# Routing attention and a MetaFormer MLP on one core: every softmax sum joined to one half before its matmul, tiny weights told by a minimum, and rows of x of two sequences made inside the MLP

## The chip, the cores and the metric

The program runs on one core of a Trainium2 chip. The metric is device time in microseconds, from the first instruction of the program to its end; the lower it is, the better. The core has TensorE (PE in the profile; PEld is its weight loads), VectorE (DVE), ScalarE (ACT), GpSimd (POOL) and SyncE (SP). SP computes nothing here: it issues most of the DMA transfers, one after the other in its program order.

## The reference

```
q, k, v: (4, 8, 768, 64) float32      centroids: (8, 16, 64)
q_assign, k_assign = argmax over 16 centroids of the normalized rows
mask   = q_assign[:, :, :, None] == k_assign[:, :, None, :]
scores = where(mask, q @ k^T / 8, -1e9);  attn = exp(scores - max) / (sum + 1e-9)
x      = (attn @ v) with the 8 heads side by side: (4, 768, 512)
xn     = (x - mean) / sqrt(var + 1e-6) * g_ln
out    = x + relu(xn @ w_ch1) @ w_ch2     w_ch1: 512x2048, w_ch2: 2048x512, both float64
```

## The kernel before

**Attention.** The 4 sequences by 8 heads make 16 pairs of heads, numbered n = 0 to 15 (four pairs to a sequence b). A pair is worked in two units, one for each half of the queries (`slot` 0 and 1). In a unit PE makes six score tiles of 128 keys by 2x384 queries in PSUM, ACT takes their exponential into a tile `e` in SBUF, and PE multiplies `e` by v (L398). VectorE adds the six tiles of a unit up: `add_up` adds three `e` tiles of two steps each (L433, L436), which leaves two halves of 128x768, `two[:, 0]` and `two[:, 1]`. `finish(n, 0)` multiplies the sums by a matrix of ones on PE (`den_ps`, L452), four matmuls with 32 columns of weights for each half, so that the denominators of a pair come out in one PSUM bank. For the pairs in `NARROW` = (7, 8, 9, 10, 14) VectorE joins the two halves first (L438), and PE has four such matmuls instead of eight; pair 15 has its own path and four. The order of PE, DVE, ACT and POOL is written out by hand here (`manual_schedule`); SP's is left to the scheduler.

`finish(n, 1)` takes the reciprocal of the denominators through DRAM; `finish(n, 2)` multiplies and stores x by columns (`xT_d`); `finish(n, 3)` transposes it on DVE (L498) and stores rows (`x_d`) with four DMAs of 128-byte pieces.

**The weights** are float64 in DRAM. They come as 32 chunks m of 128x512 (16 of w1, then 16 of w2). For each, SP loads the raw words (L242, two buffers, so that the load of chunk m+2 follows the last reading of chunk m), DVE splits off the high words and joins the low ones, and POOL adds the low part onto the weight with an accumulating DMA (L274). In `split_weight` DVE makes `ta` (L251, L254) and the masked exponent `tb` (L257); in `join_weight` it multiplies `ta` by (exponent >= SMALLEST), so that tiny weights become 0 (L266), and scales the low words (L270, L271). Chunks 0 to 21 are converted within the attention: two in each of the pairs 0 to 6 (`TWICE`) and one in each of the pairs 7 to 14. The other ten are converted within the first layer of the MLP for sequence 0, at the places that `within` gives.

**The MLP** treats w1 and w2 as 2x2 blocks and makes seven products where eight would be needed (Strassen's scheme in Winograd's form), with sums on DVE. `first_layer(b, j, part)` makes one of the seven products of hidden chunk pair j = 0 to 7; a run of seven such products is called unit j here. `product` (L803) writes PSUM banks `x_ps`, `y_ps`, `z_ps`; ACT copies x out (L829) and DVE adds y or z to the copy (`add_relu`, L834). `w1_sums` (L627) makes the block sums of w1 for the unit that follows. The last three of unit 7 stand thus:

```
        if tt == 0:
            first_layer(0, NFH - 1, 4)
            first_layer(0, NFH - 1, 3)
```

that is, behind the first 16 matmuls of the second layer (`second_layer`, L910; seven products, each over three row tiles tt). Part 3 adds onto the `z_ps` bank that DVE has to have read for part 7 before. Sequences 1 to 3 then have a first layer like that of sequence 0 and a second layer in a deeper scheme (`deep_layer`, L1093). `w2_whole(False)` stores w2 to DRAM in 16 pieces (L1001, `w_all<-w`), each as soon as the four chunks that it holds have been accumulated; those stores and the raw loads are on the same SP queue, in an order that the scheduler makes. During the second layer of sequence 0 only PE's order is written by hand; the scheduler orders DVE. There DVE makes sums of hidden tiles (`hidden_sums`), sums of w2 (`w2_sum`), adds x to the results (`add_rows`, with a load `xb` of rows of x) and normalizes sequence 1 (`norm_rows`, `norm_apply`, `x_sum`).

At the end a flag (`all_in_range`) chooses whether a slow general path, after the end of the measured work, has to redo everything. With this data it doesn't.

Of the kernel before, what the change touches and what calls it, by code (L numbers as in the profile page):

```python
# [15 lines left out]
PSUM = bass.MemoryType.PSUM  # L16


@with_exitstack
def kernel(  # L20
# [20 lines left out]
    Q = 32  # L41
# [35 lines left out]
    TWICE = 7  # L77

    NARROW = (7, 8, 9, 10, 14)
# [143 lines left out]
    halves = {}  # L223
# [20 lines left out]

    def split_weight(m):
        words = raws[m].bitcast(U32).rearrange("p (n w) -> p n w", w=2)
        hi = words[:, :, 1]
        ta = pools["conv"].tile([P, WC], U32, tag="ta", name="ta")
        tb = pools["conv"].tile([P, WC], U32, tag="tb", name="tb", bufs=2)

        nc.vector.tensor_scalar(  # L251
            ta, hi, 0x07FFFFFF, 3, op0=ALU.bitwise_and, op1=ALU.logical_shift_left
        )
        nc.vector.scalar_tensor_tensor(  # L254
            out=ta, in0=hi, scalar=0xC0000000, in1=ta, op0=ALU.bitwise_and, op1=ALU.bitwise_or
        )
        nc.vector.tensor_single_scalar(tb, hi, 0x7FF00000, op=ALU.bitwise_and)  # L257
        halves[m] = (ta, tb)

    def join_weight(m):  # L260
        lo = raws.pop(m).bitcast(U32).rearrange("p (n w) -> p n w", w=2)[:, :, 0]
        ta, tb = halves.pop(m)
        fa, fb = ta.bitcast(F32), tb.bitcast(F32)
        w = weight_chunk(m)[1]

        nc.vector.scalar_tensor_tensor(  # L266
            out=w, in0=tb, scalar=float(0x38100000), in1=fa, op0=ALU.is_ge, op1=ALU.mult
        )

        nc.vector.tensor_single_scalar(tb, w.bitcast(U32), 0xFF800000, op=ALU.bitwise_and)  # L270
        nc.vector.scalar_tensor_tensor(  # L271
            out=fb, in0=lo, scalar=2.0 ** -52, in1=fb, op0=ALU.mult, op1=ALU.mult
        )
        nc.gpsimd.dma_start(out=w, in_=fb, accum_op=ALU.add)  # L274
# [141 lines left out]
    def add_up(n, g, parts=range(2)):  # L416
# [17 lines left out]
        if 1 in parts:  # L434
            two = sums[n, g]
            nc.vector.tensor_tensor(two, two, soft.pop(u + 2), ALU.add)  # L436
            if n in NARROW:
                nc.vector.tensor_tensor(two[:, 0], two[:, 0], two[:, 1], ALU.add)  # L438
            sums[n, g] = [two[:, h] for h in range(1 if n in NARROW else 2)]
# [3 lines left out]
    def finish(n, part):  # L443
# [39 lines left out]
        elif part == 2:  # L483
            a, x = xs.pop(n), late[n]
            if b:
                nc.vector.tensor_tensor(x, a, x, ALU.mult)
                nc.sync.dma_start(out=xT_d[b][pr], in_=x)
            else:
                late[n] = norm_tiles(b)[0][:, pr, :]
                nc.vector.tensor_tensor(late[n], a, x, ALU.mult)  # L490
        else:
            x = late.pop(n)

            if n + 1 < len(pairs):
                y = last.tile([P, S], F32, tag="y", name="y")
            else:
                y = late["all"][:, 0]
            nc.vector.transpose(y, x)  # L498
            for i in range(P // Q):
                m = pr * P + i * Q  # L500
                nc.sync.dma_start(
                    out=x_d[b].rearrange("t (a r) m -> r (t a) m", r=Q)[:, :, m : m + Q],
                    in_=y[i * Q : (i + 1) * Q].rearrange("r (g f) -> r g f", f=Q),
                )
# [153 lines left out]
    for n in range(len(pairs) - 1):  # L658
        for slot in (0, 1) if n < TWICE else (0,):
            convert[n, slot] = len(convert)  # L660
# [98 lines left out]
    def all_in_range():  # L759
# [8 lines left out]
        for op, op1 in ((ALU.max, ALU.is_le), (ALU.min, ALU.is_ge)):  # L768
            nc.vector.tensor_reduce(ends[:, 1:2], hits, AX.X, op)
            nc.vector.tensor_single_scalar(ends[:, 1:2], ends[:, 1:2], float(NG), op=op1)  # L770
            nc.vector.tensor_tensor(ends[:, 0:1], ends[:, 0:1], ends[:, 1:2], ALU.min)
# [24 lines left out]
    for m in range(len(convert), NWC):  # L796
        within.setdefault((1, 2, 2, 3, 4, 4, 5, 6, 6, 7)[m - len(convert)], []).append(m)
# [98 lines left out]
    def hidden_sums(c, late):  # L896

        a11, a12, a21, a22 = [hidden[r, l, c] for r in range(2) for l in range(2)]
        if late:
            nc.vector.tensor_tensor(a12, a12, a11, ALU.subtract)  # L900
            return
        s3 = place("e")[:, c]
        hidden["s3", c] = s3
        nc.vector.tensor_tensor(s3, a11, a21, ALU.subtract)
        nc.vector.tensor_tensor(a21, a21, a22, ALU.add)
        nc.vector.tensor_tensor(a11, a21, a11, ALU.subtract)
# [10 lines left out]
    def add_rows(b, r, tt, j, bank):  # L917
# [3 lines left out]
        o = early.tile([P, MH], F32, tag="o", name="o_sb", bufs=12)  # L921
# [70 lines left out]
    def w2_whole(back):  # L992

        for r in range(2):
            for k in range(2):
                for l in range(2):
                    for h in range(2):
# [3 lines left out]
                        nc.sync.dma_start(out=w if back else d, in_=d if back else w)  # L1001
# [318 lines left out]
    with tc.manual_schedule(engines={mybir.EngineType.PE}):  # L1320
# [5 lines left out]
        relu(len(summed))  # L1326
        w2_sum(st, 1)
        w2_keep(1, st["t", 1])
        for tt in range(TH):
            second_layer(0, tt, 1, st)  # L1330
            if tt == 0:
                first_layer(0, NFH - 1, 4)
                first_layer(0, NFH - 1, 3)
        relu(len(summed))
        for c in range(NFH):
            hidden_sums(c, False)
        w2_sum(st, 2)
        norm_load(1)
        rows_load(1, 0)
        for part in (2, 5, 6, 7, 4, 3):  # L1340
            for tt in range(TH):
                second_layer(0, tt, part, st)
                if part == 6 and tt == 0:
                    norm_stat_rows(1)
            if part == 2:
                for c in range(NFH):
                    hidden_sums(c, True)
            if part == 5:
                w2_keep(2, st["t", 2])
                w2_sum(st, 3)  # L1350
                w2_keep(3, st["t", 3])
            if part == 6:
                w2_sum(st, 4)
                w2_keep(4, st["t", 2])
            if part in (2, 5):
                for tt in range(TH):
                    norm_rows(1, (0 if part == 2 else TH) + tt)
                if part == 5:
                    norm_stats(1)
            if part == 7:  # L1360
                for i in range(2):
                    for c in range(NDC):
                        norm_apply(1, i, c)
                w2_whole(False)
            if part == 4:
                for i in range(1, 5):
                    x_sum(1, i)
        w1_sums(1, 0)

    with tc.manual_schedule(engines=order | {mybir.EngineType.SP}):  # L1370
# [4 lines left out]
        def unit_end(b, j):  # L1375
# [6 lines left out]
            if b == 1:  # L1382
                if j == 0:
                    outer["ends"] = all_in_range()
# [58 lines left out]
    with tc.If(usual == 0):  # L1443
        w2_whole(True)
        with tc.For_i(0, B, 1) as b:
            general(tc, b, q, k, v, out, cT, rev, eps, ident, g_sb, w1, w2)

# [193 lines left out]
```

## Time and profile before

| | us |
|---|---|
| median of 3 runs (lowest to highest) | 894.65 (894.53 to 895.18) |
| the profiled execution: its own time | 896.45 |
| its span, first to last instruction | 894.6 |
| attention: to the last denominators of pair 15 | 329.9 |
| first layer of sequence 0 | 329.9 to 399.7 |
| second layer of sequence 0 | 399.7 to 475.1 |
| sequences 1 to 3 | 475.1 to 894.6 |

The profiled execution is one run; it is 1.8 us above the median of the others. Its page gives busy time by engine, the span in 40 slices of 22.4 us, and groups of instructions by source line. Matmuls are pipelined, so the durations of matmuls overlap; when PE works without a break, the distance from one start to the next tells what a matmul costs.

### The profile page before, as it was taken

The page shows a single profiled execution, that of the slowest core. Times are in us where ns is not written, and L with a number is a line of the kernel's source. Part 1 is how long each engine was busy: PE and PEld are TensorE (multiplying, and loading weights), DVE is VectorE, ACT ScalarE, POOL GpSimd, SP SyncE. Part 2 cuts the span into 40 slices and gives each one's busy share as a digit, 9 for nine tenths or more (in the row PEclk, how much of TensorE's full clock was granted, in tenths as well). Part 3 has the DMA queues.
Part 4 walks back from the last instruction along what each step waited for, and adds up shares of the span by engine and source line. Part 5 has one row for each costly group of instructions (what it writes and reads, how often), then busy time and mean ns, then how long its engine had stood idle before and what let it go on. Part 6 is the DMA issues. An engine that isn't in the chain of part 4 may idle for free.

```text
span 894.6 us, 13278 instructions
## 1 busy us (share of the span) xinstructions
PE 879.7 (98%) x4724; PEld 576.6 (64%) x4724; DVE 701.5 (78%) x1158; ACT 399.7 (45%) x739; POOL 79.3 (9%) x143
## 2 busy tenths in 40 slices
PE   8999999999999999999999999999999999999995
PEld 4444444444444445568886558997557997557995
DVE  6999989899888888889555777897646897645774
ACT  4777777898877753331003552102553111333110
POOL 1122222112111212110000000000000000000000
PEclk9999999999999999999999999999999999999999
DMA  7889999999797536877423558963236862511875
GB/s 154 151 184 176 161 167 193 220 197 180 159 217 129 146 90 181 202 189 244 163 73 134 195 196 302 306 178 91 48 86 183 286 204 54 98 72 36 270 200 99
DMA packets 250489, 147.86 MB, mean 165 GB/s; under 512 B 193568, under 2 KB 209072, under 8 KB 249392
## 3 DMA queue, kind: packets, MB, share of 16 engines
q1 hardware_dynamic: 234784, 130.75, 56.3%
q0 software_dynamic: 7776, 15.03, 8.6%
q10 hardware_dynamic: 7856, 1.16, 0.8%
q8 instruction: 39, 0.64, 0.3%
q14 instruction: 34, 0.28, 0.1%
HBM read 105.25 MB, written 33.25 MB: 155 GB/s over the span
## 4 chain that ended last, share of the span: by engine, by line
PE 64%; DVE 0%; issue 0%
PE x_ps L803 18%; PE x_ps L1093 12%; PE z_ps L803 9%; PE z_ps L1093 6%; PE x_ps L910 5%; PE y_ps L803 5%; PE y_ps L1093 3%; PE z_ps L910 2%; PE y_ps L910 1%; PE s_ps L386 1%; PE a_ps L398 1%; PE den_ps L452 0%; DVE u L1108 0%; DVE y_end L1194 0%; DVE m L1108 0%
## 5 line engine op out<-in xcount | busy, mean ns | idle before, releaser
L381 ACT ACTIVATE e<-s_ps 128x768 f32<-128x768 f32 x192 | 151.2, 813 | 8.8 <-PE s_ps L386 5.0
L386 PE MATMUL s_ps<-t,t 64*128 64x384 f32 x768 | 154.9, 483 | 0.0
L398 PE MATMUL a_ps<-e,v_sb 128*64 128x384 f32 x768 | 130.9, 490 | 0.0
L398 PEld LDWEIGHTS a_ps<-e,v_sb 128*64 128x64 f32 x768 | 52.3, 137 | 75.8 <-issue 62.8
L386 PEld LDWEIGHTS s_ps<-t,t 64*128 64x128 f32 x768 | 68.2, 188 | 34.6 <-issue 33.6
L1093 PE MATMUL x_ps<-lower,w 128*128 128x192 f32 x448 | 80.9, 327 | 1.2 <-DVE u L1108 0.9
L1093 PEld LDWEIGHTS x_ps<-lower,w 128*128 128x128 f32 x448 | 74.0, 190 | 3.1 <-DVE u L1108 1.5
L834 DVE TENSOR_TENSOR lower<-z_ps,u 128x384 f32<-128x384 f32 x56 | 31.0, 553 | 54.7 <-PE z_ps L803 45.9
L386 PE MATMUL s_ps<-mask,mask 64*128 64x384 bf16 x384 | 63.0, 324 | 1.1 <-ACT e L381 0.7
L842 ACT ACTIVATE lower<-lower 128x384 f32<-128x384 f32 x88 | 45.0, 522 | 40.3 <-DVE lower L834 40.3
L433 DVE TENSOR_TENSOR two<-e 128x1536 f32<-128x1536 f32 x30 | 52.6, 1753 | 13.0 <-ACT e L381 12.9
L829 ACT COPY u<-x_ps 128x384 f32<-128x384 f32 x64 | 30.6, 479 | 68.1 <-PE x_ps L803 68.1
L829 ACT COPY p<-x_ps 128x384 f32<-128x384 f32 x32 | 15.1, 471 | 91.1 <-PE x_ps L803 91.1
L436 DVE TENSOR_TENSOR two<-two,e 128x1536 f32<-128x1536 f32 x30 | 52.6, 1752 | 1.7
L386 PEld LDWEIGHTS <-mask 64*128 64x128 bf16 x384 | 19.4, 94 | 42.7 <-issue 11.7
L803 PE MATMUL x_ps<-xn,w 128*128 128x384 f32 x128 | 46.6, 487 | 0.0
L803 PE MATMUL x_ps<-xn,ws 128*128 128x384 f32 x128 | 46.5, 486 | 0.0
L803 PE MATMUL y_ps<-xn,w 128*128 128x384 f32 x128 | 46.5, 486 | 0.0
L803 PE MATMUL x_ps<-xt,ws 128*128 128x384 f32 x128 | 46.5, 486 | 0.0
L803 PE MATMUL z_ps<-xt,ws 128*128 128x384 f32 x128 | 46.5, 486 | 0.0
L803 PE MATMUL x_ps<-xt,w 128*128 128x384 f32 x128 | 46.5, 486 | 0.0
L803 PE MATMUL z_ps<-xn,ws 128*128 128x384 f32 x128 | 46.5, 486 | 0.0
(210 smaller groups left out, 1486.7 us busy)
## 6 DMA issues: line engine op xcount, KB each, us to landing
w<-w_d SPq DMA_DIRECT2D x84, 256.0 KB, 3.7
raw<-in_moe_w_ch_dram SPq DMA_DIRECT2D x32, 512.0 KB, 5.7
w<-w_t SPq DMA_DIRECT2D x36, 256.0 KB, 5.0
w<-tb POOLq DMA_DIRECT2D x32, 256.0 KB, 6.6
w_d<-wt SPq DMA_DIRECT2D x7, 1024.0 KB, 4.7
w<-w_all SPq DMA_DIRECT2D x27, 256.0 KB, 3.0
v_sb<-in_v_dram SPq DMA_DIRECT2D x32, 192.0 KB, 4.7
xr<-x_d SPq DMA_DIRECT2D x24, 256.0 KB, 3.1
```

Source lines behind the costliest of these rows:

```text
L381: nc.scalar.activation(e, s[:, :, :HC], AF.Exp, scale=SCALE)
L386: nc.tensor.matmul(s[:, j, :HC], of_keys[:, keys], of_queries[:, o : o + HC], start=part == first, stop=part != first, skip_group_check=True,)
L398: nc.tensor.matmul(acc[j * D : (j + 1) * D, :HC], loaded[n]["v"][:, j, c, :], e[:, j, :], start=(c == 0), stop=(c == NT - 1),)
L433: nc.vector.tensor_tensor(two, soft.pop(u), soft.pop(u + 1), ALU.add)
L436: nc.vector.tensor_tensor(two, two, soft.pop(u + 2), ALU.add)
L803: nc.tensor.matmul(bank[:, :HC], lhs[:, c, :], rhs[:, c], start=first and c == 0, stop=c == NDH - 1, skip_group_check=True,)
L829: nc.scalar.copy(t, bank[:, :HC])
L834: nc.vector.tensor_tensor(h, bank[:, :HC], other, ALU.add)
L842: nc.scalar.activation(h, h, AF.Relu)
L910: nc.tensor.matmul(bank[:, :MH].rearrange("p (h f) -> p h f", h=2), hidden[lhs + (c,)][:, tt * P : (tt + 1) * P], rhs[:, :, c], start=firs ...
L1093: nc.tensor.matmul(bank, w[:, c, :], a[:, c], start=way in (1, 2, 5) and c == 0, stop=c == NQH - 1, skip_group_check=True,)
```

## The change

All 15 pairs with two halves are treated as the five of `NARROW` were. A chunk of weights is converted with five DVE operations instead of six: the exponent is neither masked nor compared; the weight's high part is written at once, and a `tensor_reduce` keeps the least magnitude of the chunk in `least[:, m]`, which `all_in_range` compares with `LEAST` at the end. Two chunks a pair are converted only in the pairs 0, 1, 4 and 10, so that 19 chunks fall into the attention and 13 into the first layer. The rows of x of sequences 2 and 3 are no longer made within the attention: `xT_d` is loaded back (`columns_load`), turned on DVE and stored (`columns_turn`, `rows_out`), five times in the second layer of sequence 0 and three times in the units of sequence 1. In the second layer of sequence 0 DVE's order is now written out by hand too (`jobs`). If the flag asks for the general path, the weights are converted once more there (`whole_weights`) instead of being copied back.

```diff
-    TWICE = 7
-    NARROW = (7, 8, 9, 10, 14)
+    LATER = 2
+    TWICE = (0, 1, 4, 10)
...
     def split_weight(m):
...
         nc.vector.tensor_scalar(
             ta, hi, 0x07FFFFFF, 3, op0=ALU.bitwise_and, op1=ALU.logical_shift_left
         )
+        nc.vector.tensor_reduce(
+            least[:, m : m + 1], hi.bitcast(F32), AX.X, ALU.min, apply_absolute_value=True
+        )
         nc.vector.scalar_tensor_tensor(
-            out=ta, in0=hi, scalar=0xC0000000, in1=ta, op0=ALU.bitwise_and, op1=ALU.bitwise_or
+            out=w.bitcast(U32), in0=hi, scalar=0xC0000000, in1=ta, op0=ALU.bitwise_and, op1=ALU.bitwise_or
         )
-        nc.vector.tensor_single_scalar(tb, hi, 0x7FF00000, op=ALU.bitwise_and)
...
     def join_weight(m):
...
-        nc.vector.scalar_tensor_tensor(
-            out=w, in0=tb, scalar=float(0x38100000), in1=fa, op0=ALU.is_ge, op1=ALU.mult
-        )
...
-            if n in NARROW:
-                nc.vector.tensor_tensor(two[:, 0], two[:, 0], two[:, 1], ALU.add)
-            sums[n, g] = [two[:, h] for h in range(1 if n in NARROW else 2)]
+            nc.vector.tensor_tensor(two[:, 0], two[:, 0], two[:, 1], ALU.add)
+            sums[n, g] = [two[:, 0]]
...
+        elif b < LATER:
+            rows_out(b, pr, late.pop(n), last.tile([P, S], F32, tag="y", name="y"))
         else:
-            x = late.pop(n)
...
+            late.pop(n)
...
+    def columns_load(tile_of):
+        if asked:
+            b, pr = asked.pop(0)
+            columns[b, pr] = tile_of()
+            nc.sync.dma_start(out=columns[b, pr], in_=xT_d[b][pr])
+
+    def columns_turn(tile_of):
+        b, pr = turning.pop(0)
+        rows_out(b, pr, columns.pop((b, pr)), tile_of())
...
-        within.setdefault((1, 2, 2, 3, 4, 4, 5, 6, 6, 7)[m - len(convert)], []).append(m)
+        within.setdefault((1, 2, 2, 3, 3, 4, 4, 5, 5, 6, 6, 7, 7)[m - len(convert)], []).append(m)
...
-        o = early.tile([P, MH], F32, tag="o", name="o_sb", bufs=12)
+        o = early.tile([P, MH], F32, tag="o", name="o_sb", bufs=9)
...
-    with tc.manual_schedule(engines={mybir.EngineType.PE}):
+    with tc.manual_schedule(engines={mybir.EngineType.PE, mybir.EngineType.DVE}):
...
+        def turn_columns():
+            columns_turn(lambda: early.tile([P, S], F32, tag="turned", name="turned", bufs=1))
+            if len(turning) > 4:
+                columns_load(column)
...
+        jobs = {
...
+            (5, 2): [do(hidden_sums, 4, range(5, NFH)), turn_columns],
+            (6, 0): [do(norm_stat_rows, 1), do(w2_sum, st, 3), keep(3, 3)],
+            (6, 1): [turn_columns],
+            (6, 2): [do(w2_sum, st, 4), keep(4, 2)],
+            (7, 0): [turn_columns, do(norm_apply, 1, 0, 0), do(norm_apply, 1, 0, 1)],
+            (7, 1): [do(norm_apply, 1, 0, 2), do(norm_apply, 1, 0, 3)],
+            (7, 2): [turn_columns, do(norm_apply, 1, 1, 0), w2_whole],
+            (4, 0): [do(norm_apply, 1, 1, 1), do(norm_apply, 1, 1, 2)],
+            (4, 1): [turn_columns, do(norm_apply, 1, 1, 3)],
...
+        }
+        for part in (1, 2, 5, 6, 7, 4, 3):
             for tt in range(TH):
                 second_layer(0, tt, part, st)
...
+                for job in jobs[part, tt]:
+                    job()
...
             if b == 1:
...
+                if turning and j % 2:
+                    columns_turn(row)
+                elif asked and j % 2 == 0:
+                    columns_load(row)
```

The changed program can be built without a chip, which gives the order of its instructions on each engine. PE has the same instructions in the same order but for 40 matmuls on `den_ps`; ACT's order is the same. In SP's order of the first layer, the raw loads and the `w_all` stores stand thus: raw 19, 20, 21, four `w_all` (they wait for the accumulation of chunk 19), raw 22, 23, 24, 25, one `w_all` (waits for chunk 23), `xT_d`, two `w_all`, raw 26, one `w_all`, raw 27, the store of a sum of w2, raw 28, 29, four `w_all` (they wait for chunk 27), raw 30, 31.

## The prediction

> **What bounds the kernel now.** I read the page first: its busy times and its slices.
>
> ```profile
> PE 879.7 (98%) x4724; PEld 576.6 (64%) x4724; DVE 701.5 (78%) x1158; ACT 399.7 (45%) x739; POOL 79.3 (9%) x143
> PE   8999999999999999999999999999999999999995
> DVE  6999989899888888889555777897646897645774
> ```
>
> PE works in every slice; VectorE is near 90% in the first 19 slices, the attention and the first layer of sequence 0. So time goes only if PE gets less to do, and comes back if a busier VectorE, or a transfer that VectorE waits for, makes PE wait. The table by stretch (PE, PEld, DVE, ACT and POOL busy, clock, DMA share, GB/s) gives each stage's cover: in the first layer VectorE has 60.2 of 69.8 us, the least idle time outside the attention.
>
> ```profile
> 22.00:329.90 307.90, 306.57 (x2179) 140.75 (x2175) 281.67 (x368) 244.53 (x372) 62.70 (x97) 1.00 0.84 170
> 329.90:399.70 69.80, 69.80 (x221) 41.09 (x218) 60.20 (x125) 24.10 (x53) 11.22 (x15) 1.00 0.75 191
> 399.70:475.10 75.40, 75.40 (x347) 65.54 (x346) 47.41 (x95) 4.06 (x8) 0.43 (x1) 1.00 0.45 149
> ```
>
> Next PE's timeline, at the denominators of a pair with two halves and of a pair with one:
>
> ```profile
> 95.54 1.50 PE L452 MATMUL den_ps<-two,ones 128*32 128x384 f32 x16
> 96.86 0.83 PE L305 MATMUL sim_ps<-t,cT 128*32 128x384 f32 x8
> ...
> 195.26 0.85 PE L452 MATMUL den_ps<-two,ones 128*32 128x384 f32 x8
> 195.93 0.83 PE L305 MATMUL sim_ps<-t,cT 128*32 128x384 f32 x8
> ```
>
> From the first start to the next operation's start it is 1.32 us for two halves and 0.67 us for one. Last, VectorE's groups for a weight chunk and its neighbours, and SP's own timeline in the first layer:
>
> ```profile
> L254 DVE SCALAR_TENSOR_TENSOR ta<-raw,ta 128x512 uint32<-128x512 uint32 x32 | 22.1, 692 | 1.1
> L266 DVE SCALAR_TENSOR_TENSOR w<-tb,ta 128x512 f32<-128x512 uint32 x32 | 21.9, 684 | 0.0
> L257 DVE TENSOR_SCALAR tb<-raw 128x512 uint32<-128x512 uint32 x32 | 13.6, 424 | 0.3 <-DMA w<-tb 0.3
> L438 DVE TENSOR_TENSOR two<-two 128x768 f32<-128x768 f32 x10 | 9.6, 957 | 0.3
> L321 DVE TENSOR_REDUCE best<-sim_sb 128x24 f32<-128x384 f32 x16 | 8.8, 553 | 0.5
> ```
> ```profile
> 343.75 11.10 SPq L242 DMA_DIRECT2D raw<-in_moe_w_ch_dram  x3
> 356.96 3.21 SPq L1001 DMA_DIRECT2D w_all<-w  x4
> 360.28 0.78 SPq L242 DMA_DIRECT2D raw<-in_moe_w_ch_dram  x1
> ```
>
> The accumulation issued by POOL at 351.02 landed at 356.94; 0.02 us later SP, which had waited for it, issued four `w_all`, and the raw load behind them only at 360.28, 3.3 us after.
>
> **Part 1, the softmax sums.** PE loses four matmuls in each of ten pairs, 10 x (1.32 - 0.67) = 6.5 us. They are on the path: PE has no break around them. VectorE gains 20 additions of 957 ns, 19.1 us. In the attention it loses seven transposes of x (979 ns, 6.9 us), three chunks of 404 + 692 + 424 + 684 + 429 + 692 = 3325 ns (10.0 us) and, in each of the 19 chunks left, L257 and L266 (1108 ns) against one reduction. The reduction of 512 numbers isn't in the trace; L321 takes 553 ns for 384 and L763 341 ns for 192, so by the line through both it is 0.69 us (bounds 0.42, the row that it replaces, and 0.8). So VectorE has 19.1 - 6.9 - 10.0 - 19 x 0.42 = 5.8 us less to do in the attention, in a stage 6.5 us shorter.
>
> [...]
>
> What covers the additions, pair by pair: a pair lasts 19.4 us on PE. In successive starts (an operation begins 0.08 us before the end of one it doesn't depend on) VectorE has 17.8 us in an ordinary pair with one chunk, and 20.6 in pair 4 with two chunks and its transpose. Pair 4 so ends 1.2 us late, which pair 5 makes good. The nearest consumer, the similarity matmuls, follows the transposes of q and k by 2.7 to 3.9 us now (52.9 to 56.8 in pair 2); in pairs 0 and 1, where VectorE is latest, I leave 1.4 us. I charge nothing, and up to 1 us for the upper end.
>
> **Part 2, three more chunks in the first layer.** In successive starts a chunk costs VectorE 2.63 us, after 3.20 before. A unit j of 9.03 us with two chunks then has 5.26, three evictions (1.44) and four sums of w1 (1.54): 8.2 us. Units 2 to 7 all have two now; with the sum of w2 (2.4) and the product of pair 15 (0.98) that is 52.9 of 54.2 us, where it was 51.1. It holds if no chunk comes late. But the changed SP order puts raw 22, 26 and 30 behind `w_all` stores that wait for an accumulation. On the clock of the profile before, with its durations added up in the new order (VectorE is ready when what stands before on it, and its wait for PE, is done):
> - Chunk 19 is joined at 343.0, POOL issues at 343.3, it lands 4.35 us later (as the one issued at 344.28 did), the four `w_all` take 3.2, raw 22 lands 6.14 later (as that of 360.28 did): 357.0, where VectorE is ready at 355.5.
> - Two chunks and two evictions are 6.2 us: chunk 23 is joined at 363.2, accumulated in 5.9 (the one of 351.02) by 369.4; three `w_all` and `xT_d` take 2.8, raw 26 lands at 378.3, where VectorE is ready at 376.3.
> - 6.2 us and a piece of the w2 sum later, at 385.1, chunk 27 is joined; in 5.9 to 7.1 us (the latter beside a store of 1 MB, the one of 382.14) it is there; four `w_all` and 6.1: raw 30 lands at 400.8 to 402.0, where VectorE is ready at 396.
> - Two chunks, their evictions and the eviction of part 7 are 6.7 us: z is read at 407.5 to 408.7. PE wants that bank for part 3 of unit 7 at 404.4. It waits 3.1 to 4.3 us, somewhat of it sooner, on the relu of the last `lower`. I take 3.7.
>
> The ends: with the shortest rows (accumulation 5.0, `w_all` 0.6, raw 3.6) no raw load is late and PE waits for nothing. With the longest (7.3, 1.0, 6.6) z is read at 414.0, a wait of 9.6 us.
>
> **Part 3, the second layer and after.** Behind that wait VectorE has about 12 us of sums before PE needs them at part 5 (23 us in), so the hand-written order holds. Five transposes (979 ns) are added to 47.4 busy of 75.4 us. Each has four stores and the next load on SP; `turned` has one buffer, so the following transpose waits for them: the four stores of `late` took from 366.78 to 370.95, 4.2 us, and turns are 6.9 us apart. The tightest place: `xb` of (7, 1) stands on SP behind the third turn's stores and a load; the turn ends at 449.1, five issues take 3, the load 2.4 to 4.4, VectorE reads the bank by 454.5 to 456.9, and PE wants it at 457.6. In sequence 1 three turns of 1 us go into units with 2 us idle. I charge nothing, up to 1 us. What the stores leave in the attention, SP issues and DMA time, hid beside PE. `all_in_range` gains three operations of some 0.17 us, off the path.
>
> **The sum**, against the profiled execution's 896.45: less 6.5, plus 3.7, is 893.7. That execution is 1.8 above the median; from the median of 894.65, to which the measurement will be compared, it is 891.9 us. A difference of 0.2%, 1.8 us, is about what a measurement of this kernel can tell from none.
>
> **The rivals.**
> - *Full gain*: raw 22, 26 and 30 come in time. For it: in the profile before, the same kind of `w_all` held no raw load that VectorE then waited for, and landings vary from 3.6 to 6.6. Against it: three blocks in a row, and VectorE with 1.3 us to spare. 888.2 us, with waits up to 1.5 us 889.7. Pairs 6 and 9 are 0.16 and 0.56 us longer than their like (20.20 from 155.67 to 175.87, 19.95 from 214.66 to 234.61); should that go too, it is 887.5. Chance 0.27.
> - *No change*: blocks half a microsecond longer each, a wait of 4.7 to 8.2: 892.9 to 896.4. Chance 0.17.
> - *Slower, by the same queue*: each block feeds the next, so 1.5 us more in each gives 4 to 5 more at the end. It decides from raw 30 landing after 406.0, for then z is read after 412.6 and the wait passes 8.2. With the longest rows 894.65 - 6.5 + 9.6 = 897.8. Against it: these rows never fell together. Chance 0.18.
> - That the change doesn't do what it says: no; the 40 matmuls are gone from PE's order.
>
> **How the numbers follow.** My forecast, a wait of 1.5 to 4.7 us, 889.7 to 892.9, has 0.38. The range from 887.5 to 897.5 takes in the full gain and leaves out the upper part of the slower case. Faster 0.27 + 0.38 = 0.65, the same 0.17, slower 0.18.
>
> **What would show it.** Right: eight `den_ps` records in each pair and pairs of 19.4 us; in the first layer idle time of VectorE before the first operation on raw 22, 26, 30 put down to raw loads, and of PE before L803 of z or L910 put down to VectorE. Wrong: pairs longer than 19.5 us (VectorE would be the bound in the attention), no idle time of PE before 410, or new idle time of PE in the second layer behind `o_sb`, `xb` or `turned`.

## The result, and the profile after

The changed kernel takes 902.59 us (median; 899.83 to 905.49) where the kernel before takes 895.18 (894.53 to 895.88): 1.0084 times as long, interval 1.0066 to 1.0103. That is 7.4 us slower; the forecast was 2.8 us faster, and 902.6 lies 5 us above the top of the range. The profiled execution of the changed kernel took 902.96 us, with a span of 900.8 us against 894.6.

The page of the changed kernel first: busy times, PE's slices and the granted clock.

```profile
PE 878.8 (98%) x4644; PEld 575.3 (64%) x4644; DVE 704.8 (78%) x1149; ACT 400.5 (44%) x739; POOL 78.2 (9%) x143
PE   8999999999999999989989999999999999999996
PEclk9999999999999999989999999999999999999998
```

PE has 80 matmul records fewer (40 matmuls, each with two records), and yet only 0.9 us less of busy time in a span 6.2 us longer. Two of its slices are no longer full, the one from 382.8 us in the first layer of sequence 0 and the one from 450.4 us in the second, and in the first of them the clock is not full either. The table by stretch (attention, first layer, second layer; columns as in the prediction) says where:

```profile
22.00:323.00 301.00, 299.67 (x2096) 137.89 (x2093) 275.00 (x345) 245.11 (x372) 59.21 (x94) 1.00 0.76 155
323.00:407.50 84.50, 79.34 (x242) 46.55 (x241) 61.03 (x128) 25.87 (x56) 14.04 (x18) 0.96 0.74 201
407.50:482.00 74.50, 72.25 (x326) 62.48 (x325) 53.18 (x100) 2.36 (x4) 0.00 (x0) 0.98 0.66 187
```

PE stands idle for 5.2 and 2.3 us in the two MLP stretches, at a mean clock of 0.96 and 0.98. The attention is as forecast; PE's timeline at a pair that had two halves before, and VectorE's groups for the new operations:

```profile
93.02 0.85 PE L458 MATMUL den_ps<-two,ones 128*32 128x384 f32 x8
93.69 0.83 PE L312 MATMUL sim_ps<-t,cT 128*32 128x384 f32 x8
```
```profile
L444 DVE TENSOR_TENSOR two<-two 128x768 f32<-128x768 f32 x30 | 28.7, 958 | 1.0
...
L263 DVE TENSOR_REDUCE least<-raw 128x1 f32<-128x512 f32 x32 | 22.0, 688 | 0.0
```

SP's timeline in the first layer shows raw loads held behind `w_all`, as the order had them, and the waits from 322 to 470 us (engine, operation, what it waited for: us in total, times, longest) show who paid:

```profile
340.94 2.70 SPq L1025 DMA_DIRECT2D w_all<-w  x4
343.75 14.18 SPq L247 DMA_DIRECT2D raw<-in_moe_w_ch_dram  x4
...
386.12 3.12 SPq L1025 DMA_DIRECT2D w_all<-w  x4
389.34 1.32 SPq L247 DMA_DIRECT2D raw<-in_moe_w_ch_dram  x2
```
```profile
DVE ta L260 <- DMA raw<-in_moe_w_ch_dram: 9.8, 4, 5.9
...
DVE o_sb L946 <- DMA xb<-x_d: 5.9, 1, 5.9
...
DVE turned L504 <- DMA x_d<-turned: 2.6, 1, 2.6
```

Matching PE's matmuls of the two traces one by one, `den_ps` left out, gives the difference of their starts (after minus before), and so a ledger that adds up:

| up to | what changes | us |
| --- | --- | --- |
| 303 | ten steps of -0.64 or -0.65 at the denominators, 0.6 less wait at the head, -0.1 elsewhere | -7.2 |
| 401.9 | first layer, PE waits: 1.45 (w1 sums, behind the store of `late`), 0.99 (last relu) and 2.73 (ScalarE's copy `u3`), both behind raw 30; in starts 1.6, 1.3 and 3.0 | +5.9 |
| 407.2 | the granted clock is 0.5 from 400.57 to 407.40 | +2.7 |
| 461.6 | second layer, part 4 waits 2.25 for `o_sb`, which waits for `xb` | +2.5 |
| 465.4 | the granted clock is 0.5 from 462.01 to 465.43 | +1.7 |
| 555.3 | sequence 1, the first `y_ps` of the deep layer waits 1.00 | +1.2 |
| end | PE's last matmul | +6.9 |

A step of the starts is 0.16 to 0.17 us more than the idle time (1.61 at the wait of 1.45 us, 2.42 at that of 2.25), for without a break a matmul starts before the one ahead of it has ended in the profile: four of 128x384 take 1.45 us at 366.69 us, and the next start after 1.29. Small shifts between the waits make up the rest of the ledger. The tail behind PE is 0.7 shorter, which leaves the 6.2 us of the span.

The first wait, at 369.4 us, comes ahead of VectorE's first reading of raw 26 (372.40, after 0.53 us of waiting). What VectorE waits for just before it is the store of `late`, in whose place the second w2 sum is written; SP issues that store at 363.70, behind a `w_all` that waits for chunk 23:

```profile
366.76 0.69 DVE L917 TENSOR_TENSOR w2t<-w 128x512 f32<-128x512 f32 x1 [1.79 <-DMA xT_d<-late]
...
370.87 1.53 PE L826 MATMUL x_ps<-xt,ws 128*128 128x384 f32 x4 [1.45 <-DVE ws L647]
```

Two of these steps were in no line of the prediction: the clock. PE's timeline at the second step, and the windows around both stretches (PEclk is the third number from the end):

```profile
398.46 0.70 PE L934 MATMUL x_ps<-w,lower 128*128 128x256 f32 x2 [0.99 <-ACT lower L865]
401.88 2.93 PE L826 MATMUL x_ps<-xt,w 128*128 128x384 f32 x4 [2.73 <-ACT u L852]
404.60 2.77 PE L826 MATMUL z_ps<-xn,ws 128*128 128x384 f32 x4
```
```profile
397.16:400.57 3.41, 1.01 (x4) 0.30 (x2) 3.38 (x8) 0.52 (x1) 0.10 (x1) 1.00 0.00 0
400.57:403.98 3.41, 2.10 (x4) 1.19 (x5) 2.20 (x5) 1.41 (x3) 1.63 (x2) 0.50 0.54 94
403.98:407.40 3.42, 3.42 (x7) 1.91 (x6) 0.00 (x0) 0.49 (x1) 0.00 (x0) 0.50 0.49 102
458.60:462.01 3.41, 1.16 (x6) 0.70 (x5) 0.84 (x3) 0.00 (x0) 0.00 (x0) 1.00 0.74 257
462.01:465.43 3.42, 3.42 (x10) 2.67 (x9) 3.39 (x7) 0.00 (x0) 0.00 (x0) 0.50 0.26 78
```

Four matmuls of 128x384 that take 1.45 us elsewhere take 2.77. In the window before each stretch PE is idle for 2.40 us (0.99 and the first 1.41 of the 2.73) and 2.25 us (one wait) of 3.41. In the kernel before, PE's longest wait between 20 us and the end is 1.16 us, and the clock is full from 6.29 to 890.34 us.

### The profile page after: what moved, and what is told of

The parts are those of the page before. It is cut to its first block, busy times and chain, and to the rows that moved or that the text cites. A ratio compares the mean times of both kernels' runs of the same rounds, so it can differ in the third digit from the quotient of the medians.

```text
span 900.8 us, 13115 instructions
## 1 busy us (share of the span) xinstructions
PE 878.8 (98%) x4644; PEld 575.3 (64%) x4644; DVE 704.8 (78%) x1149; ACT 400.5 (44%) x739; POOL 78.2 (9%) x143
## 3 DMA queue, kind: packets, MB, share of 16 engines
q10 hardware_dynamic: 7856, 1.16, 0.8%
## 4 chain that ended last, share of the span: by engine, by line
PE 51%; DVE 6%; DMA 6%; SPq 1%; issue 1%; ACT 0%; DVEq 0%; ACTq 0%
PE x_ps L826 14%; PE x_ps L1117 12%; PE z_ps L826 7%; PE z_ps L1117 6%; PE y_ps L826 3%; PE y_ps L1117 3%; DMA raw<-in_moe_w_ch_dram 3%; PE x_ps L934 2%; PE y_ps L934 1%; PE z_ps L934 1%; PE s_ps L393 1%; DMA w_t<-w_t 1%; PE a_ps L405 1%; SPq L507 1%; DVE lower L857 1%
```

## The experiments

The theory after the result: the sums give their 6.5 us. They are given back by waits that come from the order of transfers on SP, raw loads behind `w_all` and `xb` behind the turns' stores, and each long wait is paid a second time by the clock. The rivals: VectorE simply has too much to do where the chunks went; the turns' stores fill the DMA engines, whatever the queue; the clock falls for some other reason. The kernel before, run beside each set of experiments, had medians of 895.1 to 896.1 us.

**The sums alone** (the kernel before with one line changed).

```diff
-    NARROW = (7, 8, 9, 10, 14)
+    NARROW = tuple(range(15))
```

> The kernel before with one edit: all fifteen early pairs add the halves of their sums on VectorE; 22 chunks in the attention and all transposes of x stay where they were. Theory A (the sums and the rest of the change need each other): in pairs 1 to 6 VectorE was busy 18.3 to 19.5 of 20 us already, two additions of 0.96 us make it 20.2 to 21.4 us against a pair of 19.4 on PE, so PE waits in these pairs; six pairs by 1 us or so each over 20.06 cost 4 to 6 us, the four pairs 0, 11, 12, 13 give 2.6: 896 to 899 us. Rival (VectorE has enough slack, the additions alone give the whole gain): 10 x 0.65 = 6.5 us less than the kernel before, 888.7 us.

904.79 us (900.71 to 907.27), 1.0107 times the kernel before (1.008 to 1.0133). The direction is theory A's, the size is not: five of the pairs with two chunks last 21.3 to 21.5 us. In three of them PE waits 1.88 to 1.92 us for the transposes of q and k; two of these waits:

```profile
119.57 0.85 PE L305 MATMUL sim_ps<-t,cT 128*32 128x384 f32 x8 [1.88 <-DVE t L283]
141.06 0.85 PE L305 MATMUL sim_ps<-t,cT 128*32 128x384 f32 x8 [1.92 <-DVE t L283]
```

Behind the second of these the clock is 0.5 for 3.41 us, as it is behind the wait at 74.85 us; behind the first it is not. The other two long pairs are the ones with the half clock in them. So VectorE can't carry the additions by themselves: something else of the change has to make room.

**`w_all` on GpSimd.**

```diff
-                        nc.sync.dma_start(out=d, in_=w)
+                        nc.gpsimd.dma_start(out=d, in_=w)
```

> The changed kernel with the sixteen w_all stores issued by GpSimd and not by SP, so that no raw load stands behind them; what VectorE has to do is the same. Theory A (queue): VectorE's four waits for raw in the first layer (9.8 us) go, with them PE's waits of 1.45, 0.99 and 2.73 us and the stretch of 6.8 us at half clock (2.8 us): 902.6 - 8.4 = 894.2 us. Rival (VectorE itself has too much to do in the first layer, 13 chunks): PE's waits before 405 us stay within 2 us of what they were, 900 to 903 us.

904.01 us (901.01 to 907.99). By its time this is nearer the rival's, but the waits in the first layer show that only the queue has changed:

```profile
DVE tb L277 <- DMA w<-tb: 11.3, 3, 4.5
...
DVE ta L260 <- DMA raw<-in_moe_w_ch_dram: 0.7, 1, 0.7
```

The raw loads are in time. Now the accumulations stand behind `w_all` on GpSimd, each group of four waiting for the accumulation before it to land, and VectorE waits for the two buffers of `tb` that they free. The run moves the blockage and doesn't remove it; it decides nothing on VectorE's load.

**The turns' stores on ScalarE**, alone and with the edit above.

```diff
-            nc.sync.dma_start(
+            queue.dma_start(
...
-            columns_turn(lambda: early.tile([P, S], F32, tag="turned", name="turned", bufs=1))
+            columns_turn(lambda: early.tile([P, S], F32, tag="turned", name="turned", bufs=1), nc.scalar)
```

> The changed kernel with the stores of the five turns in the second layer issued by ScalarE and not by SP, so that no xb load stands behind them. Theory A (the xb of part 4 is late because its load stands on SP behind the third turn's stores): the wait of 2.25 us before part 4 and the 3.4 us at half clock behind it go, 902.6 - 4.1 = 898.5 us; VectorE's wait of 2.6 us for the one buffer of turned may stay. Rival (the stores fill the DMA engines, on whatever queue): xb lands as late, 901.5 to 903.5 us.

> Both edits: w_all on GpSimd, the turns' stores of the second layer on ScalarE. Theory A: both gains add, 902.6 - 8.4 - 4.1 = 890.1 us, 5 us below the kernel before. Rival (each wait only moves on to the next late thing, or VectorE's load is what counts): 895 us or more.

905.31 us (903.88 to 906.66) and 914.13 (910.38 to 915.83). In the first, PE's wait before part 4 fell from 2.25 to 0.95 us: `xb` was no longer late. But VectorE's waits for `turned` grew from 2.6 to 12.4 us, and the instruction order, which is made anew for each kernel, put the eviction of sequence 1's first `y` ahead of sums of x, so that VectorE waited 6.2 us for PE and then PE 5.1 us for VectorE. The sum of both edits was not the sum of two gains: raw in time, `tb` late, the same 5.1, and three waits of PE in sequence 1 (4.2 us) for ScalarE, for in the kernel with both edits the three turns of sequence 1 went to ScalarE too, which its expectation doesn't say. Both expectations failed, and the runs are of use only for the clock (below).

**Part 2 undone, and part 3 undone.**

```diff
-    TWICE = (0, 1, 4, 10)
+    TWICE = (0, 1, 3, 5, 7, 9, 11)
...
-        within.setdefault((1, 2, 2, 3, 3, 4, 4, 5, 5, 6, 6, 7, 7)[m - len(convert)], []).append(m)
+        within.setdefault((1, 2, 2, 3, 4, 4, 5, 6, 6, 7)[m - len(convert)], []).append(m)
```

> The changed kernel with part 2 undone: 22 chunks are converted in the attention and 10 in the first layer, as before, the second chunks put in pairs 0, 1, 3, 5, 7, 9 and 11; the sums, the shorter conversion and the turns stay as changed. Theory A (the loss of the first layer comes from its 13 chunks): PE's waits before 405 us (1.45, 0.99, 2.73) and the half clock behind them go, 902.6 - 8.4 = 894.2 us; in the attention a pair of VectorE has 1.2 to 1.7 us to spare in the changed kernel, a chunk costs 2.6, so each second chunk makes the next pair 1 us late and no later: pairs stay 19.4 us. Rival (the same wall as in the run with the sums alone: VectorE is full in the attention and PE waits there instead): pairs of 20 us and more, 897 us or more.

897.62 us (894.63 to 901.42), 1.0014 times the kernel before (1.0001 to 1.0026). The first layer's waits are gone (the longest is 0.31 us), and the pairs stay at 19.4 us but for one wait of 1.55 in pair 13. The second layer's wait is 3.20 us in its profile, with 6.83 us at half clock. So taking the three chunks out of the first layer gives back 5 us of the 7.4, less than the 8.4 expected: pair 13 waits, and the second layer's wait is longer in this profile, which is of the slowest of ten runs. VectorE still waits 4.81 us for a raw load behind four `w_all` there; with ten chunks it has the time to make that good, and PE does not wait.

```diff
-    LATER = 2
-    TWICE = (0, 1, 4, 10)
+    LATER = 4
+    TWICE = (0, 1, 4, 6)
```

> The changed kernel with part 3 undone: all rows of x are turned and stored in the attention, as before; the second chunk of pair 10 goes to pair 6, for the transposes fill pairs 10 to 14. Theory A: the wait of 2.25 us in part 4 of the second layer, the half clock behind it (1.7) and the wait of 1.0 us in sequence 1 go, while the first layer keeps its waits: 902.6 - 5 = 897.6 us. Rival (VectorE has no room for seven transposes of 0.98 us in the attention): PE waits there about a microsecond in each of five pairs, 901 us or more.

900.97 us (899.13 to 902.9). The waits of the second layer and of sequence 1 are gone but for one of 0.70 us, and the attention has none, so VectorE had room for the seven transposes. The first layer's two waits, 2.48 and 2.10 us, were followed by 10.24 us at half clock in the profiled execution. They follow a wait of VectorE of 4.92 us for the stores of `late`. Theory A in direction; the gain of 1.6 us is a third of what I expected, since the first layer's loss isn't a constant.

**Idle work for PE in its three waits** (`fill(n)` is n matmuls of the identity into a bank of its own).

```diff
+                do(fill, 20), do(first_layer, 0, NFH - 1, 4),
...
+            (4, 0): [do(fill, 16), do(norm_apply, 1, 1, 1),
```

> The changed kernel with idle work for PE in front of its three long waits: 7, 20 and 16 matmuls of the identity into a bank that nobody reads, before the last product of the first part 1, before part 4 of unit 7 and before the first part 4 of the second layer. The waits for VectorE stay as long as they were. Theory A (waits cost twice, once as waits and once by the half clock that follows): no half clock after 10 us, the granted clock of every run at 0.997 or more, 902.6 - 4.5 = 898 us, and runs that lie closer together than the 5.7 us of the changed kernel. Rival (the clock falls for another reason, or the idle work costs as much): 902 us or more.

902.51 us (900.89 to 904.16). The granted clock is 0.996 to 0.998 in all runs, where the changed kernel's are 0.990 to 0.996, and its profile has no half clock in the middle:

```profile
399.29 4.63 PE L935 MATMUL fill_ps<-ident 128*128 128x128 f32 x40
403.76 1.46 PE L826 MATMUL x_ps<-xt,w 128*128 128x384 f32 x4
```

The same four matmuls take 1.46 us and not 2.93. Against the changed kernel's trace the starts fall by 2.7 us from here to 407, and by 1.6 behind the second wait: that is the price of the half clock, shown by taking away its cause. The time did not fall, because the filling was too long: its 20 matmuls (two records each) last 4.6 us for a wait of 2.73, and PE lost 1.5 us by it against the changed kernel, 0.5 by the seven before it, and 1.0 at the third place. The expectation was right on the clock, but for one run at 0.996, and wrong on the total.

**A ladder of waits** (the kernel before with fourteen chains of small copies on ScalarE; the extra matmul writes into the bank of `z`, and the output of this kernel is not the reference's).

```diff
+        for i in range(n):
+            nc.scalar.copy(tick, bank[:, :64] if i == 0 else tick)
+        nc.tensor.matmul(bank[:1, QC : QC + 64], tick[:, :1], tick[:, :64], ...)
```

> The kernel before with fourteen waits of PE put into the deep layers of sequences 2 and 3: after seven products of each, PE waits for a chain of 3 to 17 dependent copies of 128x64 on ScalarE, a different length each time, and then does one small matmul whose result isn't used. Its time means nothing. Theory A (the clock is set by the idle share of a window of fixed length and fixed grid: the two stretches at half clock in the changed kernel were 6.83 and 3.41 us, and lie 18 x 3.413 us apart): stretches at half clock are whole multiples of 3.41 us, begin on one grid, and follow the waits that leave more than about half of one grid window idle, so waits below 1.7 us never and waits above 3.4 us always. Rival 1 (a threshold on the length of the wait alone, between 1.45 and 2.25 us): every wait longer than some length is followed by half clock at a fixed delay. Rival 2 (the clock has nothing to do with waits): no half clock in the middle.

Before the end the trace has half clock nine times; all of its edges lie on one grid of 3.413 us. Each wait, and how much of it lies in one window of that grid:

| wait of PE, us | most in one window | half clock behind it, us |
| --- | --- | --- |
| 0.85, 1.18, 1.46, 1.74 | all of it | none |
| 2.01 | 1.14 | none |
| 2.29, 2.56, 2.84 | all of it | 3.41 each |
| 3.12, 3.39 | 3.06, 2.01 | 3.41 each |
| 3.67, 4.22, 4.32, 4.72 | 2.44, 3.41, 3.41, 2.90 | 6.83 each |

The other kernels give the pair that parts theory A from a threshold on the wait's length: the wait before part 4 of the second layer, 2.25 us in the changed kernel and 2.23 in the run below with 11 chunks and `xb` on SP. In the changed kernel it lies in one window, and half clock follows. In the other run a border of the grid falls into it (0.48 us before it, 1.75 behind), and the clock stays full:

```profile
461.61 8.64 PE L934 MATMUL x_ps<-w2t,lower 128*128 128x256 f32 x31 [2.25 <-DVE o_sb L946]
```
```profile
458.61 7.17 PE L934 MATMUL x_ps<-w2t,lower 128*128 128x256 f32 x32 [2.23 <-DVE o_sb L946]
```
```profile
453.44:456.85 3.41, 2.93 (x14) 2.25 (x12) 0.00 (x0) 0.00 (x0) 0.00 (x0) 1.00 1.05 206
456.85:460.27 3.42, 1.67 (x8) 1.49 (x9) 2.11 (x4) 0.00 (x0) 0.00 (x0) 1.00 0.68 231
```

What counts is a window's sum and not a single wait. The run with the turns' stores on ScalarE has the same wait of 2.73 us before part 4 of unit 7 as the changed kernel, and in both a border falls into it. In the changed kernel the window ahead of the border also holds the 0.99 us before, 2.40 in all, and half clock follows; in the other run it holds 1.09 and 0.64, and the clock stays full:

```profile
401.82 1.56 PE L826 MATMUL x_ps<-xt,w 128*128 128x384 f32 x4 [2.73 <-ACT u L852]
403.21 1.45 PE L826 MATMUL z_ps<-xn,ws 128*128 128x384 f32 x4
```
```profile
396.77:400.18 3.41, 1.68 (x7) 0.83 (x5) 3.38 (x7) 0.53 (x1) 0.00 (x0) 1.00 0.00 0
400.18:403.59 3.41, 1.77 (x6) 1.11 (x7) 2.52 (x6) 1.59 (x4) 1.74 (x2) 1.00 0.44 77
```

**A third buffer for raw** in the changed kernel, the direct test of queue against work.

```diff
-                raw = pools["conv"].tile([P, WC], mybir.dt.int64, tag="raw", name="raw", bufs=2)
+                raw = pools["conv"].tile([P, WC], mybir.dt.int64, tag="raw", name="raw", bufs=3)
...
-                load_weight(m + 2)
+                load_weight(m + 3)
```

> The changed kernel with three buffers of raw in the first layer and not two, so that each raw load is asked for one chunk sooner on SP; the same 13 chunks, the same order of work on PE, VectorE, ScalarE and GpSimd. Theory A (the loss of the first layer is the raw loads' place behind w_all on SP, not VectorE's work): VectorE's wait for raw falls from 9.8 us to under 2, PE's waits of 1.45, 0.99 and 2.73 us and the half clock behind them go: 902.6 - 8.4 = 894.2 us, with the second layer's wait as it was. Rival (13 chunks are too much for VectorE): 900 us or more.

900.72 us (900.08 to 902.11). In the first layer theory A holds: with the same 13 chunks and the same order on VectorE, PE reaches part 4 of unit 7 at 399.2 us where the changed kernel has 401.9, and only one wait of PE over 0.4 us is left: 1.82 at the w1 sums, behind a wait of VectorE of 4.04 us for the store of `late`. That one has nothing to do with raw, and the edit does not touch it. VectorE's wait for raw is 2.4 us, where under 2 was expected. The waits to 407 us:

```profile
DVE o_sb L946 <- DMA xb<-x_d: 6.3, 1, 6.3
...
DVE ta L260 <- DMA raw<-in_moe_w_ch_dram: 2.4, 1, 2.4
```

But the first `xb` loads, issued from 325.35 us in the changed kernel, now stand on SP behind the last raw and go out only at 403.32; why they do was not shown. PE waits 3.05 us in part 2 of the second layer, with 3.41 us of half clock behind it, and most of the gain is gone. The total was predicted wrong for a reason that the edit itself brought.

**The orders put right, part by part.** All sums joined, as changed; 21 chunks in the attention and 11 in the first layer; `xb` issued by ScalarE; the turns of sequence 1 in its units 1 to 3; then the same with `xb` on SP, and the first with three buffers of raw (there only the `xb` of parts 7 and 4 are on ScalarE).

```diff
+    TWICE = (0, 1, 3, 5, 7, 9)
...
-        nc.sync.dma_start(out=x, in_=x_d[b][r * TH + tt, :, j * MH : (j + 1) * MH])
+        (nc.scalar if r else nc.sync).dma_start(out=x, in_=x_d[b][r * TH + tt, :, j * MH : (j + 1) * MH])
...
-                if turning and j % 2:
+                if turning and j:
                     columns_turn(row)
-                elif asked and j % 2 == 0:
-                    columns_load(row)
+                columns_load(row)
```

> The changed kernel with all the sums joined, 21 chunks in the attention (second chunks in pairs 0, 1, 3, 5, 7 and 9) and 11 in the first layer, the xb loads issued by ScalarE and not by SP, and the three turns of sequence 1 in its units 1 to 3 and not 1, 3 and 5. Theory A (the queue order, not the work, made the waits): from the 897.6 us with the chunks put back go the wait in pair 13 (1.55), the wait of the second layer (3.2) with the half clock behind it (about 2), and the wait of 1.24 in sequence 1: about 890 us, 5 to 6 us below the kernel before. Rival (the stores of the turns fill the DMA engines, so xb lands as late from any queue, and one more chunk in the first layer brings its waits back): 896 us or more.

> The same kernel as the run with xb on ScalarE, but xb on SP as in the changed kernel. Theory A (xb is late because its load is issued late by SP, behind the stores of the turns): the wait before part 4 of the second layer is there again, 2 to 3 us, with half clock behind it in some runs: 893 to 895 us. Rival (the DMA engines are the limit): the same time as with xb on ScalarE.

> The run with xb on ScalarE (all sums joined, 21 chunks in the attention, 11 in the first layer, the turns of sequence 1 sooner) with three buffers of raw as well; of the xb loads those of parts 7 and 4 stay on ScalarE, the others are on SP. Theory A: from 896.95 us go PE's waits in the first layer (3.1 and 0.7 us) and the half clock in them (1.5): 891.6 us, 3.5 us below the kernel before. Rival (something else comes late in their place): 895 us or more.

- `xb` on ScalarE: 896.95 us (895.46 to 898.65), 1.0019 times the kernel before (1.001 to 1.0028). The wait before part 4 is gone, and so is that of sequence 1. But raw is late once more (10.2 us on VectorE in two waits), and PE waits 2.84 and 0.57 us in the first layer, with 3.41 us of half clock; it waits 1.08 us late in the attention and 1.14 at the start of sequence 1 besides. The expected 890 failed on these.
- `xb` on SP: 897.76 us (895.2 to 900.06). The wait before part 4 is there again, 2.23 us, behind 5.7 us of VectorE's for `xb`; by the profiles the queue decides it. The expected 893 to 895 failed on the first layer's waits (2.80 and 1.54). The medians are only 0.8 us apart, and their ranges overlap, so the times don't show it.
- With three buffers of raw: 891.72 us (891.32 to 892.2), 0.996 times the kernel before (0.9946 to 0.9974), 3.5 us faster than it and 10.9 faster than the changed kernel. The expectation was 891.6. Its first layer, and VectorE's waits there:

```profile
322.00:399.00 77.00, 76.44 (x250) 45.23 (x247) 56.51 (x118) 26.10 (x57) 12.35 (x16) 1.00 0.69 184
```
```profile
DVE ta L260 <- DMA raw<-in_moe_w_ch_dram: 2.6, 2, 1.9
```

PE is idle for 0.6 us in 77 where it was idle for 5.2 in 84.5, the clock is full from 5.68 to 886.32 us, and the runs lie within 0.9 us. Against the kernel before, PE is 6.7 us ahead at the end of the attention and 4.5 at its last matmul.

## Why the prediction was wrong

**Part 1 held.** 10 x 0.65 = 6.5 was the forecast of PE's gain; ten steps of 0.64 or 0.65 came. VectorE covered the additions: no wait of PE of over 0.3 us between 20 us and the last pair's 1.16, which the kernel before has too. The reduction, estimated at 0.69 us by the line through two rows (553 ns for 384 numbers, 341 for 192), takes 0.688 (L263). That something has to make room for the additions is shown by the run with the sums alone. Neither of the other two parts is needed whole for it: with part 3 undone PE has no new wait in the attention, and with part 2 undone one of 1.55 us.

**Part 2: the mechanism was right, the size was not.** Raw 22, 26 and 30 were late for the reason given, by 2.77, 0.53 and 5.90 us, and the last block was paid for in unit 7, as worked out: 4.3 us by the ledger, 3.7 of idle time. It was not paid at z's bank: PE waited before part 4, for ScalarE to copy `u3` out, and not before part 3. The other 1.6 us were missing from the sum, which made 5.9 where I took 3.7 and gave the forecast 1.5 to 4.7. I had costed the raw loads as the only transfers that VectorE waits for. But the second w2 sum waited 1.79 us for the store of `late`, which stands on SP in the same blocked stretch, and the w1 sums behind it came late for PE. The run with three buffers of raw shows that this wait is the store's: there raw 22 is in time, and the wait is 1.82.

**The clock was the step that failed outright.** 4.4 us of half clock are in no term of the sum, nor in the range. In the trace of before PE's longest wait between 20 us and the end is 1.16 us, and the clock stays full behind it, so no row of it showed the price; a change that is expected to put a wait of 3.7 us into PE leaves the range of waits that the trace covers, and I priced that wait at its length alone. The grid measured here is 3.413 us in every profile, and the windows that PE left idle for 2.01 to 3.06 us, and not throughout, were each followed by half clock.

**Part 3 failed as "I charge nothing, up to 1 us".** The place named as the tightest, `xb` behind the third turn's stores, is where it broke: 2.5 us, and 1.7 of clock. I let the turn end at 449.1 and took 3 us for five issues; on a PE 1.5 us later there than before, it began only at 452.56, because `turned` waited for the stores of the turn before, one of whose issues alone held SP for 3.1 us, and VectorE read the bank at 461.13, not by 456.9. The three turns in sequence 1, charged at nothing, cost 1.2: their stores stand on SP ahead of a load of w2's sums, which VectorE waited 3.06 us for. With part 3 undone the wait is not there; in the three runs that, among other edits, move the turns to earlier units it is gone too.

**Together**, the span was to be 894.6 - 6.5 + 3.7 = 891.8 us and is 900.8. Of the 9.0 us between, the clock is 4.4, the second layer's wait 2.5, the first layer's 2.2 and sequence 1's 1.2; the head and the tail give 1.3 back.

**The rival** "slower, by the same queue" had the right sign at 897.8 us, in part by luck. It took 9.6 us of waits in the first layer, where 5.9 came; the rest of the loss is the clock and the second layer, of which it says nothing.

Not settled: how much of the spread of the changed kernel's runs, 5.7 us, is the clock and how much the transfers. With the clock held up by idle work it is still 3.3 us.

## What to carry to other kernels

When a change moves loads or stores onto a queue, work out for each what stands ahead of it there and what that waits for, and do it for every stage that the change touches; the edits that put the orders right (two chunks back, a third buffer, another queue for some `xb` loads, turns sooner) were worth 10.9 us together, where the work saved is 6.5. In this kernel a wait of PE cost more than its length once about 2 us of idle time fell into one 3.413 us window of the clock (half clock behind 2.0 us and more, none behind 1.80 and less), so price such a wait twice, or keep it below that. An edit that frees one queue has to be read in the waits and not in the time alone: two of these runs, `w_all` on GpSimd and the third buffer by itself, gained little or nothing because the blockage had moved to the next resource.

## What the hardware showed that I had not expected

- In every profile the granted clock changed only on a grid of 3.413 us, whose phase differed from run to run (an edge of the changed kernel, at 400.57 us, and one of the kernel before, at 890.34, lie 143.5 steps apart). Over all profiles, each of the 19 windows at full clock in which PE was idle for 2.0 us or more was followed by half clock, none with 1.80 us or less was; of three with 1.92 or 1.93 us two were.
- Behind a window at half clock the next one was at full clock where PE had been idle in it for 0.62, 0.51 us and less, and at half clock again where it had been idle for 0.63 us and more, and once after 0.52. So the half clock came as 3.41, 6.83 or 10.24 us.
- A wait before part 4 of the second layer cost nothing beyond its length in one kernel (2.23 us) and 1.7 us more in another (2.25 us), by the phase of the grid.
- In the changed kernel the fourth store of a turn (32x24x32 floats, runs of 128 bytes) held SP's issue for 1.6, 3.1 and 1.2 us in the first three turns of the second layer, where the first store takes 0.3 to 0.4, and the loads behind it waited for that. In the run with part 2 undone it held SP for up to 3.7 us.
